# Reordering VectorE's, ACT's and SyncE's steps in the first round of block products, at the turns between token groups, and in the loads of x

## The chip, the cores and the metric

The kernel runs on one core of one Trainium2 chip. The metric is the device time of the whole program in microseconds (us); lower is better. A core has five engines with queues of their own, each of which works through its instructions in the order in which the program lists them: TensorE (PE, matrix products; its weight loads are shown as PEld), VectorE (DVE), ScalarE (ACT), GpSimd (POOL) and SyncE (SP, which here issues the DMA transfers).

## The reference

Block-sparse attention over q, k and v (4 batches, 8 heads, 768 positions, head size 64), and a two-layer network with a squared ReLU on its result:

```python
attn = softmax(where(mask, q @ k.T / 8, -1e9))       # mask: neighbours, edge blocks, sampled blocks
x = (attn @ v).transpose(0, 2, 1, 3).reshape(3072, 512)
h = x @ w_in                                         # w_in: 512 x 2048
r = maximum(h, 0)
g = s * (r * r) + b
out = g @ w_out                                      # w_out: 2048 x 512
```

The weights come as 64-bit floats. The kernel decodes each into a high and a low 32-bit part, and a product of two such operands is three matmuls: high by high, high by low, low by high.

## The kernel before, in words

**Stages.** Attention for all four batches comes first and spills x, transposed, to a DRAM tile `xd`. While it ends, the weights are decoded. Then comes the network. The tokens are cut into eight groups of 384, g = 0 to 7, two for each batch. Groups 0 and 1 go through the plain product: for each of 16 blocks f of 128 hidden columns, `mlp1` multiplies x by `w_in`, `relu`, `square`, `hidden_high` and `hidden_low` make the hidden block as a high and a low part (on ACT, ACT, ACT and DVE here), and `mlp2` multiplies it by `w_out` and adds it up in PSUM. These are 32 hidden blocks, i = 0 to 31. `mlp1(i)` writes PSUM bank i % 2, and `relu(i)` is what reads that bank.

**Block products.** Groups 2 to 7 are taken in pairs, a stage for each pair: s = 1, 2 and 3, with a = 2s and b = 2s + 1. Here x @ w_in is done in rounds p = 0 to 7, each of which makes hidden blocks p and p + 8 of both groups by seven block products instead of eight (a scheme of Strassen's kind). A round computes its products in the order n = 1, 2, 6, 7, 5, 3, 4. Product n multiplies a weight operand by an x operand:

| n | 1 | 2 | 6 | 7 | 5 | 3 | 4 |
|---|---|---|---|---|---|---|---|
| weight | A11 | A12 | S2 | S3 | S1 | S4 | A22 |
| x | B11 | B21 | T2 | T3 | T1 | B22 | T4 |

A11 to A22 are the quarters of the weight, S1 = A21 + A22, S2 = S1 - A11, S3 = A11 - A21, S4 = A12 - S2. The T's are differences and sums of parts of x in the same way: T3 = T3 - T1, T1 = T1 - T2, T2 = T2 + T3, T4 = T2 - T4, from four raw parts that are loaded into the tiles of that name. The T's and B's are made once for a stage, the S's once for a round. The change from one stage to the next is called a turn.

The products alternate between PSUM banks 0 and 1, so each waits until the product two places before it has been read. What reads them is on DVE, apart from product 1, which ACT copies (`m1`): product 2 is added to m1 and makes a hidden block (`take`: one add on DVE, then ReLU times itself on DVE), product 6 gives the partial sum u1, product 7 the partial sum u2, product 5 a hidden block and the partial sum u3, products 3 and 4 one hidden block each. `finish` makes a hidden block's high part on ACT (two steps) and its low part on POOL (line 425, the line of `hidden_low`). `out_block` is the `mlp2` of the oldest hidden block that waits in `fifo`: nine matmuls.

**Steps.** Everything else is a step with a short name, issued by `work(p, s, "...")` in the order in which the text lists it:

- `<T1`, `<B22`: load a part of x from `xd` (SP, 384 KB)
- `+T1`, `+S1`: add or subtract (DVE, line 543 or 546 for T, 541 for S)
- `wA12`: add the two parts of a weight quarter in a tile of its own (DVE, line 550). This is done only in stage 1.
- `>A12`: write that sum back over the high part of the weights (SP, line 553, 128 KB), once the products of this round have read it. `wA12` of the next round writes the same tile and so waits for this transfer; A11 and A21 likewise have one tile, A22 has two.
- `hT1`, `hS1`, `hB22`: high part of an operand (ACT, line 565)
- `lT1`, `lS1`, `lB22`: low part of it (DVE, line 567), after the high part
- `o4`: load an output weight block back from DRAM (SP, two transfers of 256 KB)

Up to hidden block 29 a planner orders the instructions: it is given for each operation its engine, a cost, a priority and what it depends on, and lays them out as a list for each engine. The list given to `early` puts the first steps of stage 1 into that plan at the lowest priority. From hidden block 30 on the order is written out by hand, in the loops printed below. `EARLY` holds the steps behind hidden blocks 30 and 31. `FIRST` holds those of stage 1's round 0, by product. `F_NOW` and `F_NEXT` hold what the rounds of stage 1 do for themselves and for the next round, `W_NOW` and `W_NEXT` the same for the weights in stages 2 and 3 (`W_NEXT[7]` also at the end of stage 1), `X_NOW` the x operands at the start of stages 2 and 3, `X_NEXT` what each round does for the x operands of the next stage. `BEHIND` holds the writes of stage 1, `BACK` the loads of the output weights.

Of the kernel before, what the change touches and what calls it, by code (L numbers as in the profile page):

```python
# [202 lines left out]
def kernel(  # L203
# [31 lines left out]
    NFC = DFF // P  # L235
# [295 lines left out]
    def get(s, n):  # L531
        g, c2 = FROM[n]
        xload(2 * s + g, c2, xsum_of(n))

    def add(p, s, n):

        if n[0] == "S":
            a11, a12, a21, a22 = (quarter(p, s, f"A{k}") for k in (11, 12, 21, 22))
            a, b, how = {"S1": (a21, a22, ALU.add), "S2": (wsum["S1"], a11, ALU.subtract),
                         "S3": (a11, a21, ALU.subtract), "S4": (a12, wsum["S2"], ALU.subtract)}[n]  # L540
            vec.tensor_tensor(out=wsum[n], in0=a, in1=b, op=how)
        elif n == "T4":
            vec.tensor_tensor(out=xsum[n], in0=xsum_of("T2"), in1=xsum[n], op=ALU.subtract)
        else:
            b, how = {"T3": ("T1", ALU.subtract), "T1": ("T2", ALU.subtract), "T2": ("T3", ALU.add)}[n]
            vec.tensor_tensor(out=xsum_of(n), in0=xsum_of(n), in1=xsum_of(b), op=how)

    def together(p, n):
        a, b = (quarter_part(p, n, part).bitcast(F32) for part in range(2))
        vec.tensor_tensor(out=put_together(p, n), in0=a, in1=b, op=ALU.add)  # L550
# [76 lines left out]
    with ExitStack() as es:  # L627
# [498 lines left out]
        for i, (kind, b, t, x) in enumerate(slots):  # L1126
# [31 lines left out]
            for j in range(nu):  # L1158
                n, ms_ = u + j, []
# [141 lines left out]

        for deps, what in (("", "<B11"), ("", "<B21"), ("", "<T1"), ("", "<T3"), ("", "<T2"), ("", "<T4"), ("<B11", "hB11"), ("hB11", "lB11"),
                           ("<B21", "hB21"), ("hB21", "lB21"), ("", "wA21"), ("", "wA22"), ("wA21 wA22", "+S1"), ("", "wA11"), ("+S1 wA11", "+S2"),
                           ("+S2", "hS2"), ("<T3 <T1", "+T3"), ("+T3 <T2", "+T1"), ("+T1", "+T2"), ("+T2", "hT2"), ("hS2", "lS2"), ("hT2", "lT2"),
                           ("+S2", "+S3"), ("+S3", ">A21")):
            early(deps, what)
        plan.run()


    W_NOW = {0: {1: "hS4"}, 1: {1: "lS3 hS4", 2: "lA22 lS4"}}  # L1310
    W_NOW.update({p: {1: "lS4 lA22"} for p in range(2, NFC // 2)})
    W_NEXT = {p: {1: "hA11", 2: "lA11 +S1 +S2 hA12", 6: "hS2", 7: "lA12 lS2 +S3", 5: "hS3 hS1 +S4", 4: "lS1 lS3 hS4 hA22"} for p in range(1, NFC // 2 - 1)}

    W_NEXT[7] = {1: "hA11", 2: "lA11 +S1 +S2 hA12", 6: "hS2", 7: "lA12 lS2", 5: "+S3 hS1", 4: "lS1 +S4 hS3 hA22"}
    W_NEXT[0] = {1: "hA11", 2: "lA11 hA12", 7: "lA12 +S1 +S2", 5: "hS2 hS1 +S3", 4: "lS2 lS1 +S4 hS3 hA22"}
    X_NOW = {1: "lT3 hT4 hB22", 2: "lT1 lS3", 7: "lB22 lS4 lT4", 5: "lA22"}
    X_NEXT = {2: {1: "<T1 <T3 <T2 <T4"}, 4: {2: "+T3", 7: "+T1"}, 5: {2: "+T2", 7: "+T4"},
              7: {1: "<B11", 2: "<B21", 6: "hB11", 7: "lB11 hT2 hB21", 5: "lT2 hT3", 3: "<B22", 4: "lB21 hT1"}}

    FIRST = {1: "lT1 lS1", 2: "hB22 hS4 lS4", 6: "lB22", 7: "hT4 lT4"}  # L1320
    F_NOW = {p: {1: "lS4"} for p in range(1, NFC // 2)}
    F_NEXT = {1: "wA21", 2: "wA22 +S1 wA11", 7: "+S2 hS2 +S3 >A21 wA12", 5: "+S4 hS3 hS1 lS2", 4: "lS1 lS3 hS4"}
    BEHIND = {1: ">A11", 2: ">A12", 4: ">A22"}
    BACK = {2: "o4", 3: "o5", 4: "o6", 5: "o7"}
    EARLY = {30: "hT3 lT3 hS3 lS3", 31: "<B22 hT1 hS1 +T4 wA12 +S4"}
    for i in range(NPL, NSUB):
        g, f = subs[i]
        mlp1(i)
# [5 lines left out]
        hidden_low(i)  # L1334
        work(0, S0, EARLY.get(i, ""))
        if i >= NSUB - LAG:
            fifo.append((i, None))
    for s in range(S0, B):
        a, b = 2 * s, 2 * s + 1
        for p in range(NFC // 2):  # L1340
            for n in (1, 2, 6, 7, 5, 3, 4):
                to = product(p, s, n)
                i = None
                if n in (2, 4) and len(fifo) >= 3 or n == 2 and s == S0 and p == 0:
                    out_block()
                if n == 1:
                    nc.scalar.copy(part_sums["m1"], to)
                elif n == 2:
                    i = take((a, p), to, part_sums["m1"], ALU.add)
                elif n == 6:  # L1350
                    vec.tensor_tensor(out=part_sums["u1"], in0=to, in1=part_sums["m1"], op=ALU.add)
                elif n == 7:
                    vec.tensor_tensor(out=part_sums["u2"], in0=to, in1=part_sums["u1"], op=ALU.add)
                elif n == 5:
                    i = take((b, p + 8), to, part_sums["u2"], ALU.add)
                    vec.tensor_tensor(out=part_sums["u3"], in0=to, in1=part_sums["u1"], op=ALU.add)
                elif n == 3:
                    i = take((b, p), to, part_sums["u3"], ALU.add)
                else:
                    i = take((a, p + 8), part_sums["u2"], to, ALU.subtract)  # L1360
                if s == S0:
                    work(p, s, BEHIND.get(n, ""))
                    work(p, s, BACK.get(p, "") if n == 1 else "")
                    work(p, s, FIRST.get(n, "") if p == 0 else F_NOW[p].get(n, ""))
                else:
                    if p == 0:
                        work(p, s, X_NOW.get(n, ""))
                    work(p, s, W_NOW[p].get(n, ""))
                if i is not None:
                    finish(i)  # L1370
                if s < B - 1:
                    work(p, s + 1, X_NEXT.get(p, {}).get(n, ""))
                if s == S0 and p < NFC // 2 - 1:
                    work(p + 1, s, F_NEXT.get(n, ""))
                elif s < B - 1 or p < NFC // 2 - 1:
                    work((p + 1) % (NFC // 2), s + p // (NFC // 2 - 1), W_NEXT[p].get(n, ""))
                if n == 7 and len(fifo) >= 2 or n == 5 and len(fifo) >= 3:
                    out_block()
# [75 lines left out]
```

## Time and profile before

| | |
|---|---|
| time, median of 3 runs | 809.35 us (807.5, 809.35, 809.81) |
| time of the profiled execution | 807.24 us |
| its span, first to last instruction | 805.2 us |
| busy: PE, PEld | 779.0 us (97%), 674.8 us (84%) |
| busy: DVE, ACT, POOL | 606.5 us (75%), 501.5 us (62%), 174.5 us (22%) |
| mean granted TensorE clock | 0.988 of full |
| first block product (stage 1, round 0) | at 408.34 us |
| stage 2, round 0 and stage 3, round 0 | at 541.73 us and 667.90 us |

Times within the profile are counted from the span's start. The rows of the profile name an engine, the line of the kernel, the operation, the tile written and the tile read, their shapes, and how often; a bracket tells how long the engine was idle ahead of the instruction and what ended the wait. A line can be that of a helper: all block products are line 583, all `mlp2` matmuls are lines 446 to 448, `take` is lines 593 and 594, m1 is line 1347, u1, u2 and u3 are lines 1351, 1353 and 1356. Tile names are those of the memory: `m` is a block product, `h` a product of `mlp1`, `o` one of `mlp2`; the operands of the T's and B's appear as `xT`, `xB`, `xt` or `wout`, those of the S's as `wop` or `win`, sums as `sum`, `whole` or `xrest`. PE's spans overlap, so that a stretch in which it is always busy need not be one in which it works at its peak.

### The profile page before, as it was taken

To read this page: it belongs to the slowest core of one execution; us is meant where nothing else is said; L and a number is where in the kernel's file an instruction comes from. 1 tells how busy PE (TensorE), PEld (TensorE's weight loads), DVE (VectorE), ACT (ScalarE), POOL (GpSimd) and SP (SyncE) were. 2 spreads that over 40 slices of the span, in tenths; PEclk is the share of its full clock that TensorE was granted. 3 is DMA by queue.
4 is the path that set the end of the run, shared out by engine and by line. 5 is a ranking of instruction groups with operands and counts; after the bars stand their busy time and mean duration, and the time that the engine had idled before them with its cause. 6 is when DMAs were issued, how large, how long until landed. Compare 5 with 4: busy or idle time off the path is not lost.

```text
span 805.2 us, 22023 instructions
## 1 busy us (share of the span) xinstructions
PE 779.0 (97%) x8352; PEld 674.8 (84%) x8352; DVE 606.5 (75%) x1528; ACT 501.5 (62%) x1190; POOL 174.5 (22%) x404
## 2 busy tenths in 40 slices
PE   7899998999999999999988999999999999999997
PEld 6587886888887899999867899998888888999986
DVE  5476777888888999998787678678667769766662
ACT  3576777787888887787864343467345457544542
POOL 5422133222400000000002232232223222322321
PEclk9899999999999999999999999999999999999999
DMA  9999797978677433543421422024000012000002
GB/s 251 251 236 310 223 262 233 245 202 235 187 228 248 143 123 105 194 146 115 143 86 66 138 82 70 26 86 144 14 0 1 1 40 93 7 1 1 1 0 79
DMA packets 89001, 100.99 MB, mean 125 GB/s; under 512 B 11584, under 2 KB 66368, under 8 KB 88896
## 3 DMA queue, kind: packets, MB, share of 16 engines
q1 hardware_dynamic: 88896, 99.59, 41.0%
q8 instruction: 66, 1.08, 0.6%
q14 instruction: 39, 0.32, 0.1%
HBM read 80.68 MB, written 14.68 MB: 118 GB/s over the span
## 4 chain that ended last, share of the span: by engine, by line
PE 90%; DMA 4%; DVE 2%; ACT 1%; SPq 1%; issue 1%; ACTq 0%; DVEq 0%
PE m L583 21%; PE o L447 10%; PE o L448 10%; PE o L446 10%; PE t L955 9%; PE xs L1000 5%; PE s L878 5%; PE xs L1014 3%; PE s L904 3%; PE h L404 3%; PE h L406 3%; PE h L405 3%; DMA kt<-in_k_seq_dram 2%; PE xs L989 1%; PE s L892 1%; PE xs L1026 1%
## 5 line engine op out<-in xcount | busy, mean ns | idle before, releaser
L425 POOL TENSOR_TENSOR hid<-hid,hid 128x384 fp32r<-128x384 f32 x96 | 102.9, 1073 | 476.3 <-ACT hid L601 475.9
L600 ACT ACTIVATE hid<-hid,sb_b,sb_s 128x384 f32<-128x384 f32 x96 | 68.0, 709 | 152.7 <-DVE hid L594 152.7
L931 ACT ACTIVATE ptile<-ptile,nm 128x352 f32<-128x352 f32 (+2 forms) x208 | 121.0, 584 | 33.9 <-DVE nm L919 33.3
L919 DVE CUSTOM_DVE_ANT_0 ptile<-s,ms 128x352 f32<-128x352 f32 x160 | 74.3, 521 | 27.1 <-PE s L904 26.5
L838 POOL COPY kg<-kt 128x128 f32 x264 | 63.6, 294 | 137.1 <-PE s L904 124.3
L583 PE MATMUL m<-wout,win 128*128 128x384 f32 x384 | 83.7, 339 | 2.0 <-ACT hid L409 1.9
L955 PE MATMUL t<-ident,ptile 128*128 128x128 f32 x608 | 80.4, 282 | 2.8 <-ACT ptile L931 2.6
L448 PE MATMUL o<-woutr,hid 128*128 128x512 f32 x192 | 75.9, 395 | 0.0
L447 PE MATMUL o<-woutr,hid 128*128 128x512 f32 x192 | 75.8, 395 | 0.0
L446 PE MATMUL o<-woutr,hid 128*128 128x512 f32 x192 | 74.6, 389 | 0.0
L955 PEld LDWEIGHTS t<-ident,ptile 128*128 128x128 f32 x608 | 67.2, 143 | 8.7 <-ACT ptile L931 3.5
L583 PEld LDWEIGHTS m<-wout,win 128*128 128x128 f32 x384 | 69.0, 188 | 6.2 <-ACT hid L409 2.7
L959 DVE COPY pt<-t 128x384 f32<-128x384 f32 (+1 forms) x104 | 56.3, 544 | 9.2 <-PE t L955 7.4
L583 PE MATMUL m<-xT,wop 128*128 128x384 f32 x288 | 58.8, 338 | 1.5 <-DVE hid L593 1.5
L961 ACT COPY pt<-t 128x384 f32<-128x384 f32 (+1 forms) x104 | 48.3, 474 | 17.0 <-PE t L955 16.2
L594 DVE SCALAR_TENSOR_TENSOR hid<-hid 128x384 f32<-128x384 f32 x96 | 55.3, 576 | 3.3
L583 PEld LDWEIGHTS m<-xT,wop 128*128 128x128 f32 x288 | 51.3, 188 | 4.5 <-DVE hid L593 1.8
L601 ACT CAST hid<-hid 128x384 fp32r<-128x384 f32 x96 | 49.3, 514 | 7.5 <-PE o L447 0.3
L567 DVE TENSOR_TENSOR win<-sum,win 128x256 fp32r<-128x256 f32 x48 | 31.8, 662 | 22.0 <-ACT win L565 22.0
L1000 PE MATMUL xs<-v,pt 128*64 128x64 f32 x1280 | 46.5, 225 | 1.8 <-issue 1.8
L448 PE MATMUL o<-wout,hid 128*128 128x512 f32 x120 | 48.1, 401 | 0.0
L1000 PEld LDWEIGHTS xs<-v,pt 128*64 128x64 f32 x1280 | 40.7, 138 | 8.8 <-issue 2.1
(186 smaller groups left out, 1754.5 us busy)
## 6 DMA issues: line engine op xcount, KB each, us to landing
vg<-in_v_dram SPq DMA_DIRECT2D x136, 128.0 KB, 3.5
v<-in_v_sta_dram SPq DMA_DIRECT2D x40, 256.0 KB, 4.2
kt<-in_k_seq_dram SPq DMA_DIRECT2D x16, 544.0 KB, 8.2
raw_i<-in_w_in_dram SPq DMA_DIRECT2D x16, 512.0 KB, 4.8
raw_o<-in_w_out_dram SPq DMA_DIRECT2D x16, 512.0 KB, 3.2
v<-in_v_dram SPq DMA_DIRECT2D x16, 384.0 KB, 4.8
xd<-xst SPq DMA_DIRECT2D x44, 128.0 KB, 3.8
out_dram<-ob SPq DMA_DIRECT2D x20, 256.0 KB, 2.0
```

The costliest lines, as they stand in the source:

```text
L425: (eng or nc.vector).tensor_tensor(out=htile(5 + i % 3), in0=t, in1=gh.bitcast(F32), op=ALU.subtract)
L446: nc.tensor.matmul(acc, gh[:, tsl], wout(f, 0), start=first, stop=False)
L447: nc.tensor.matmul(acc, gh[:, tsl], wout(f, 1), start=False, stop=False)
L448: nc.tensor.matmul(acc, gl[:, tsl], wout(f, 0), start=False, stop=last)
L583: nc.tensor.matmul(to, w_, x_, start=(c == 0 and k == 0), stop=(c == 1 and k == 2))
L600: nc.scalar.activation(t, t, AF.Identity, bias=sb_b, scale=sb_s)
L838: nc.gpsimd.tensor_copy(kg[:, m], kts[b][:, :, bass.ds(box["js"][m], BLK)])
L919: nc.vector.tensor_tensor_reduce(out=pt[:, :w], in0=sps.pop((n, g))[:, :w], in1=msk, scale=-scale, scalar=FMAX if g == 0 else nm[:, 0:1], ...
L931: nc.scalar.activation(pt[:, :w], pt[:, :w], AF.Exp, bias=nms[n][:, last:last + 1], scale=-1.0, accum_out=dns[i][:, g, j:j + 1])
L955: nc.tensor.transpose(tp[:, c, :], src[:, c * P:(c + 1) * P], ident)
L959: nc.vector.tensor_copy(to, src)
L1000: nc.tensor.matmul(xs[rows], pt[:, c, rows], vt[:, c, hp * D:(hp + 1) * D], start=(j == 0 and c == 0), stop=False, skip_group_check=True)
```

## The change

Seven tables and three lines of the loop change; what is computed stays as it is.

- T2's split (`hT2`, `lT2`) leaves the planner's list and goes behind hidden block 31. `+T4`, `wA12` and `+S4` leave the place behind hidden block 31 and go into `FIRST`, behind product 2 (`wA12`, `+S4`) and product 6 (`+T4`).
- `FIRST` is laid out anew: nothing behind product 1; `lT1` and `lS1` behind product 2, ahead of `wA12`, `+S4`, `hS4` and `hB22`; `lS4`, `+T4`, `hT4` behind product 6; `lB22` behind product 7; `lT4` behind product 5.
- What round 0 of stage 1 does for round 1 (`F_NEXT[0]`) goes behind products 5, 3 and 4, where it was spread from product 1 on. The other rounds keep their order.
- In stage 1 the write `>A11`, `>A12` or `>A22` is issued after `FIRST` or `F_NOW`, and the loads o4 to o7 go behind product 2 instead of product 1, so behind `>A12`.
- At the turns, `lS1` and `+S4` go from the end of round 7 to round 0's product 2 of the next stage, `lS3` ahead of `lT1` there, and `hS4` from product 1 to product 6.
- The loads of T1, T3, T2 and T4 for the next stage, which stood together behind product 1 of round 2, go behind product 5 of rounds 1, 2, 3 and 4.

```diff
-                           ("+S2", "hS2"), ("<T3 <T1", "+T3"), ("+T3 <T2", "+T1"), ("+T1", "+T2"), ("+T2", "hT2"), ("hS2", "lS2"), ("hT2", "lT2"),
+                           ("+S2", "hS2"), ("<T3 <T1", "+T3"), ("+T3 <T2", "+T1"), ("+T1", "+T2"), ("hS2", "lS2"),
                            ("+S2", "+S3"), ("+S3", ">A21")):
...
-    W_NOW = {0: {1: "hS4"}, 1: {1: "lS3 hS4", 2: "lA22 lS4"}}
+    W_NOW = {0: {6: "hS4"}, 1: {1: "lS3 hS4", 2: "lA22 lS4"}}
...
-    W_NEXT[7] = {1: "hA11", 2: "lA11 +S1 +S2 hA12", 6: "hS2", 7: "lA12 lS2", 5: "+S3 hS1", 4: "lS1 +S4 hS3 hA22"}
+    W_NEXT[7] = {1: "hA11", 2: "lA11 +S1 +S2 hA12", 6: "hS2", 7: "lA12 lS2", 5: "+S3 hS1", 4: "hS3 hA22"}
...
-    X_NOW = {1: "lT3 hT4 hB22", 2: "lT1 lS3", 7: "lB22 lS4 lT4", 5: "lA22"}
-    X_NEXT = {2: {1: "<T1 <T3 <T2 <T4"}, 4: {2: "+T3", 7: "+T1"}, 5: {2: "+T2", 7: "+T4"},
+    X_NOW = {1: "lT3 hT4 hB22", 2: "lS3 lT1 lS1 +S4", 7: "lB22 lS4 lT4", 5: "lA22"}
+    X_NEXT = {1: {5: "<T1"}, 2: {5: "<T3"}, 3: {5: "<T2"}, 4: {2: "+T3", 7: "+T1", 5: "<T4"}, 5: {2: "+T2", 7: "+T4"},
               7: {1: "<B11", 2: "<B21", 6: "hB11", 7: "lB11 hT2 hB21", 5: "lT2 hT3", 3: "<B22", 4: "lB21 hT1"}}
...
-    FIRST = {1: "lT1 lS1", 2: "hB22 hS4 lS4", 6: "lB22", 7: "hT4 lT4"}
+    FIRST = {2: "lT1 lS1 wA12 +S4 hS4 hB22", 6: "lS4 +T4 hT4", 7: "lB22", 5: "lT4"}
     F_NOW = {p: {1: "lS4"} for p in range(1, NFC // 2)}
-    F_NEXT = {1: "wA21", 2: "wA22 +S1 wA11", 7: "+S2 hS2 +S3 >A21 wA12", 5: "+S4 hS3 hS1 lS2", 4: "lS1 lS3 hS4"}
+    F_NEXT = {p: {1: "wA21", 2: "wA22 +S1 wA11", 7: "+S2 hS2 +S3 >A21 wA12", 5: "+S4 hS3 hS1 lS2", 4: "lS1 lS3 hS4"} for p in range(1, NFC // 2 - 1)}
+    F_NEXT[0] = {5: "wA21 wA22 +S1", 3: "wA11 +S2 hS2", 4: "+S3 >A21 hS3 hS1 lS2 wA12 +S4 lS3 lS1 hS4"}
...
-    EARLY = {30: "hT3 lT3 hS3 lS3", 31: "<B22 hT1 hS1 +T4 wA12 +S4"}
+    EARLY = {30: "hT3 lT3 hS3 lS3", 31: "<B22 hT2 lT2 hT1 hS1"}
...
                 if s == S0:
+                    work(p, s, FIRST.get(n, "") if p == 0 else F_NOW[p].get(n, ""))
                     work(p, s, BEHIND.get(n, ""))
-                    work(p, s, BACK.get(p, "") if n == 1 else "")
-                    work(p, s, FIRST.get(n, "") if p == 0 else F_NOW[p].get(n, ""))
+                    work(p, s, BACK.get(p, "") if n == 2 else "")
...
                 if s == S0 and p < NFC // 2 - 1:
-                    work(p + 1, s, F_NEXT.get(n, ""))
+                    work(p + 1, s, F_NEXT[p].get(n, ""))
```

## The prediction

> **What bounds the kernel now.** I read the page first, then the busy time cut into rounds of block products, then the order of instructions on each engine where a round is longer than its neighbours.
>
> ```profile
> span 805.2 us, 22023 instructions
> PE 779.0 (97%) x8352; PEld 674.8 (84%) x8352; DVE 606.5 (75%) x1528; ACT 501.5 (62%) x1190; POOL 174.5 (22%) x404
> ```
>
> TensorE (PE) is the bound, so only its gaps can be won. The profiled execution took 807.24 us, 2.04 more than its span. In the stretches below the columns are length, then busy us and instructions of PE, PEld, DVE, ACT and POOL, granted clock, DMA share and GB/s. The first four are rounds p = 0 to 3 of stage s = 1; then come the first rounds after the two turns; the last two stretches hold the clock dip.
>
> ```profile
> 408.34:430.10 21.76, 16.18 (x70) 13.25 (x71) 18.24 (x35) 16.31 (x32) 3.03 (x3) 0.93 0.27 97
> 430.10:445.93 15.83, 15.83 (x80) 14.26 (x79) 10.75 (x23) 6.26 (x13) 3.60 (x5) 0.99 0.10 34
> 445.93:463.20 17.27, 15.99 (x80) 14.10 (x78) 10.45 (x22) 5.83 (x13) 3.92 (x4) 1.00 0.48 153
> 463.20:478.90 15.70, 15.70 (x79) 14.14 (x78) 11.40 (x26) 7.28 (x15) 4.53 (x5) 1.00 0.20 68
> 541.73:557.98 16.25, 16.23 (x79) 14.04 (x78) 15.43 (x29) 12.25 (x26) 4.29 (x4) 1.00 0.24 86
> 667.90:684.12 16.22, 16.20 (x80) 14.04 (x78) 15.40 (x29) 12.22 (x26) 4.28 (x4) 1.00 0.22 82
> 423.40:426.80 3.40, 1.32 (x7) 1.34 (x8) 3.33 (x9) 3.37 (x8) 0.48 (x1) 1.00 0.56 200
> 426.80:430.20 3.40, 3.40 (x10) 2.63 (x9) 2.64 (x5) 2.10 (x5) 1.62 (x2) 0.53 0.22 75
> ```
>
> A round without a gap takes 15.70 us: seven products and four output blocks. Two rows price them.
>
> ```profile
> 436.51 0.39 PE L446 MATMUL o<-wout,hid 128*128 128x512 f32 x1
> 438.59 1.23 PE L583 MATMUL m<-xT,wop 128*128 128x384 f32 x6
> ```
>
> A block is 438.59 - 436.51 = 2.08, a product (15.70 - 4 x 2.08) / 7 = 1.05. Round 0 has only three blocks (two are queued when it begins), so it should take 7 x 1.05 + 3 x 2.08 = 13.6 us. It takes 21.76: **8.2 us are lost there**, 1.6 more in round 2 (17.27 against 15.70), 0.13 in round 1 and 0.5 at each turn. That is 11.0 us in all, and nothing else that the change touches has a gap. In round 0 the idle time stands here, ahead of products 2, 7 and 4 (order 1, 2, 6, 7, 5, 3, 4), and round 1 begins in the last row:
>
> ```profile
> 411.60 1.31 PE L583 MATMUL m<-wout,win 128*128 128x384 f32 x6 [1.95 <-ACT hid L409]
> 417.71 1.32 PE L583 MATMUL m<-xT,wop 128*128 128x384 f32 x6 [1.52 <-DVE hid L593]
> 425.48 1.28 PE L583 MATMUL m<-xT,win 128*128 128x384 f32 x6 [2.12 <-DVE sum L1356]
> 430.10 2.22 PE L583 MATMUL m<-wout,win 128*128 128x384 f32 x11
> ```
>
> 1.95 + 1.52 + 2.12 = 5.6 idle; after the last, PE runs at about half clock until 430.1 (0.53 granted), which is 1.6 more; the rest is start-up around the waits.
>
> **Part 1: T2's split leaves the planned list (hT2 on ACT, lT2 on DVE).** ACT's queue, with the matmul that ends the hidden block 30 and DVE's +T3:
>
> ```profile
> 403.66 0.41 ACT L565 CAST win<-sum 128x256 fp32r<-128x256 f32 x1 [3.46 <-DVE sum L541]
> 403.81 0.33 PE L406 MATMUL h<-x,win 128*128 128x384 f32 x1
> 403.87 0.95 DVE L546 TENSOR_TENSOR sum<-sum,sum 128x768 f32<-128x768 f32 x1
> 407.06 0.83 ACT L565 CAST wout<-sum 128x768 fp32r<-128x768 f32 x1 [3.00 <-DVE sum L546]
> 407.80 0.48 ACT L409 ACTIVATE hid<-h 128x384 f32<-128x384 f32 x1
> 410.03 0.83 ACT L565 CAST xT<-sum 128x768 fp32r<-128x768 f32 x1
> 410.76 0.40 ACT L565 CAST wop<-sum 128x256 fp32r<-128x256 f32 x1
> 411.07 0.48 ACT L409 ACTIVATE hid<-h 128x384 f32<-128x384 f32 x1
> 414.34 0.47 ACT L1347 COPY xrest<-m 128x384 f32<-128x384 f32 x1
> ```
>
> hT2 (407.06) idles ACT for 3.00 us waiting for +T2, with relu 30 queued behind it, though block 30 is done at 404.14. Without it relu 30 goes at 404.2. Its block's four ACT steps take 410.03 - 407.80 = 2.23: hT3 at 406.4 (its input +T3 is there from 404.82), hS3 at 407.2, relu 31 at 407.5 (now 411.07). Product 2 waits for relu 31's bank, so the first wait goes. Then 2.23 for block 31, 0.73 for hT2 at its new place and 1.04 for hT1 and hS1: the copy of product 1 starts at 411.5 and ends at 411.95, where now it starts at 414.34. Cover for hT2: product 6, its reader, comes after product 2 and a block, at 408.15 + 2 x 1.05 + 2.08 = 412.3 (product 1 starts once the block before it ends, 0.2 sooner than now); hT2 runs 409.7 to 410.55, lT2 on DVE then 0.95 to 411.5. That is 0.8 us of slack, and the copy, which product 6's bank waits for, has 0.35.
>
> **Part 2: the order FIRST.** DVE's steps as they stand, with the start-to-start times that I use:
>
> ```profile
> 413.90 0.95 DVE L543 TENSOR_TENSOR sum<-sum,sum 128x768 f32<-128x768 f32 x1
> 414.77 0.42 DVE L550 TENSOR_TENSOR sum<-win 128x256 f32<-128x256 f32 x1
> 415.22 0.43 DVE L541 TENSOR_TENSOR sum<-sum,sum 128x256 f32<-128x256 f32 x1
> 415.57 0.95 DVE L567 TENSOR_TENSOR xT<-sum,xT 128x768 fp32r<-128x768 f32 x1
> 417.10 0.55 DVE L593 TENSOR_TENSOR hid<-m,xrest 128x384 f32<-128x384 f32 x1
> 417.69 0.56 DVE L594 SCALAR_TENSOR_TENSOR hid<-hid 128x384 f32<-128x384 f32 x1
> 418.17 0.42 DVE L567 TENSOR_TENSOR win<-sum,win 128x256 fp32r<-128x256 f32 x1
> 420.10 1.37 DVE L567 TENSOR_TENSOR xB<-xB 128x768 fp32r<-128x768 f32 x1
> 421.39 0.55 DVE L1353 TENSOR_TENSOR xrest<-m,sum 128x384 f32<-128x384 f32 x1
> ```
>
> Wide step 0.87 (413.90 to 414.77), narrow 0.35 (0.45 if the next one reads it), a product's add 0.59, its square 0.48, lB22 1.29, a partial sum 0.47. Nothing is removed here: +T4, wA12, +S4, lT1, lS1 and wA21, ahead of product 2's sum at 417.10 now, go behind it. The sum then starts when the copy lands, 412.0. From there, added up in the new order: square 412.6; lT1 413.05; lS1 413.9; wA12 414.25; +S4 414.7; u1 415.05; lS4 415.5; +T4 415.85; u2 416.75; lB22 417.2; product 5's sum 418.5; its square 419.1; u3 419.55; lT4 420.0; wA21, wA22, +S1 to 422.0; product 3's sum 422.0; wA11, +S2; product 4's at 423.9; then six narrow steps of round 1 and its lS4, and round 1's product 2 at 427.8.
>
> PE against that: products 1 and 2 at 408.15 and 409.2, block, product 6 at 412.3, product 7 at 413.4, block, product 5 at 416.6 (needs u1, 415.6: hidden). Product 3 is ready at 417.65 but needs lB22, 417.2 + 1.29 = 418.5: **0.9 idle**. Product 4 is ready at 419.6 but needs lT4, 420.0 + 0.95 = 421.0: **1.4 idle**. Then a block, and round 1 begins at 421.05 + 1.05 + 2.08 = 424.2 instead of 430.10: **5.9 us won**. ACT hides behind this: hS4 waits for +S4 to 415.15 with hB22 and product 2's finish behind it; hB22 ends at 416.3, before lB22. The last steps listed for round 1 (+S3 to hS4, now all behind product 4) are read by its products 6, 5 and 3, from 428.4 on: hidden. >A21 goes out on SP behind >A22, when product 4 ends (422.1), and must have read its tile before wA21 of round 2 writes it, near 427.5: hidden too, with 5 us for 128 KB, when 384 KB in a stack took 6.4 (below).
>
> The longest gap of 1.4 us leaves over 2 us busy in any 3.4 us, against 1.32 ahead of the dip, so I take the clock as full. The Trainium skill, "TensorE: Matmul & The Clock Gate", section "Part 1: The HAM clock gate", puts the half clock after an idle window of about 3.4 us; the trace differs, since its window of the dip follows one with 1.32 us of work in it. By the page's rule the new gaps cost no clock either.
>
> What can stretch the chain is POOL:
>
> ```profile
> 426.32 1.02 POOL L425 TENSOR_TENSOR hid<-hid,hid 128x384 fp32r<-128x384 f32 x1 [5.67 <-ACT hid L601]
> 426.50 1.25 DVE L594 SCALAR_TENSOR_TENSOR hid<-hid 128x384 f32<-128x384 f32 x1
> ```
>
> The square takes 1.25 beside POOL and 0.56 alone: 0.69 lost. Three such meetings are to be had between 417.5 and 427 (POOL follows each finish). The first is in lB22's 1.37 already; two add 1.4 to round 1's product 2, which then passes PE's need for it at 429.5 by about 0.3; **0.5 us off**, between 0 and 1.5.
>
> **Part 3: BEHIND ahead of BACK, x loads spread.** Round 2 loses its 1.57 here:
>
> ```profile
> 457.94 0.43 DVE L550 TENSOR_TENSOR sum<-win 128x256 f32<-128x256 f32 x1 [4.29 <-DMA win<-sum]
> ...
> sum<-xd SPq DMA_DIRECT2D x4, 384.0 KB, 6.4
> ```
>
> wA12 waits for the write >A12, which stands on SP behind o4's two loads and four x loads (six transfers, 2 MB). Now >A12 goes ahead of o4, and only one x load, of the round before, is in front of it. The wait goes, **1.57 won** (0 if >A12 still lands late, no more than 1.57). Round 1's 0.13 goes with the dip. o4 to o7, now behind product 2, are used two rounds later: nothing. BEHIND's swap with F_NOW's lS4 changes no queue, as one is SP's and the other DVE's. The x loads go in rounds 1 to 4; T2's and T4's first readers stand at product 7 of the next round, their issue at product 5: in round 1 these begin at 436.51 - 1.05 = 435.46 and at 438.59, so 15.70 - 3.1 = 12.6 us lie between, twice the 6.4 that four stacked loads took.
>
> **Part 4: the turns.** PE's weight load waits there:
>
> ```profile
> 547.45 0.64 PEld L583 LDWEIGHTS m<-xT,wop 128*128 128x128 f32 x4 [0.28 <-DVE wop L567]
> 555.78 0.19 PEld L446 LDWEIGHTS o<-wout,hid 128*128 128x128 f32 x1 [0.34 <-ACT ob L452]
> ```
>
> The first is lS3, now ahead of lT1 (0.87 earlier): 0.28 won at each of two turns. lS1 and +S4 move behind it, 0.7 us of DVE; DVE is 15.43 of 16.25 busy, but both leave the same round's stretch, so product 2's sum starts that much earlier and u1 where it did. hS4 at product 6 delays no ACT step that PE needs. The second wait stays. **0.56 won**, between -1.0 (u1 0.5 late each time) and 1.07.
>
> **Sum:** 5.9 - 0.5 + 1.57 + 0.13 + 0.56 = 7.7, so 807.24 - 7.7 = 799.5 against the profiled execution. That one was quicker than the three runs (807.5, 809.35, 809.81; median 809.35, which would give 801.7); the mean of the four is 808.5, hence 801.
>
> **Rivals.**
> A. All gaps close: DVE catches up and products 3 and 4 wait for nothing. Then 11.0 goes: 796.2 to 798.4. Against it: 18.24 us of DVE work in round 0, now to be done in less time.
> B. DVE becomes the bound of rounds 0 and 1. POOL's meetings fall on the chain from 412 to 424, three at 0.69, and one gap grows until the clock halves for a window (1.6 as now): 7.7 - 2.1 - 1.6 = 4.0, so 804.5. The square's 1.25 speaks for it. In the Trainium skill, "SBUF — State Buffer", section "SBUF: two separate sides", VectorE and GpSimd hold a shared port pair as an exclusive lock for a whole instruction; the square, which ends only 0.4 after POOL, agrees.
> C. Round 0 doesn't shrink, since ACT is held elsewhere ahead of relu 31 (hT3 or the output copies). Then 1.57 + 0.56 remains: 806.4. Against it: +T3 ends on DVE at 404.82. From the mean of four that is 0.26%, no change that can be told.
> D. Slower: an x load lands late. T2's and T4's readers stand in DVE's queue ahead of the sums that free PE's banks. DVE's wait of 4.29 cost PE 1.57, so PE bears 2.7; a landing above 12.6 + 2.7 = 15.3 us costs, four times over. At 18 us the 7.7 and the 2.4 of a measurable loss are used up; at 18.5 it is 813. Nothing in the 6.4 speaks for it.
>
> **How the numbers follow.** Forecast 0.57, A 0.12, B 0.19, C 0.07, D 0.05. About 0.3% (2.4 us, the spread of the runs) can be told from no change: the forecast, A and B are faster (0.88), C is the same, D slower. The range goes from A's floor, 796.5, to C's edge at 806.5; D and half of C lie outside.
>
> **What would show it.** Right: relu 31 near 407.5; round 1 beginning near 424; no clock under 0.9 after 405; round 2 at 15.7; wA12 waiting for no DMA. Wrong: PE waits ahead of products 3 or 4 above 2 us, a second half-clock window, or DVE waiting for the x loads.

## The result and the profile after

The changed kernel takes 802.75 us (median of 20 runs, 799.86 to 810.38), the kernel before 809.67 us (20 runs in turn with it, 803.91 to 812.59). The ratio is 0.9928, with a 95% interval of 0.991 to 0.9947. The medians differ by 6.9 us. 801.0 was forecast, between 796.5 and 806.5.

The profiled execution of the changed kernel took 805.12 us, with a span of 803.1: only 2.1 less than before's 805.2. But its first block product stands at 412.48, where before's stands at 408.34. Those 4.1 us belong to attention and the plain products ahead of the block products; the runs below show that they aren't the change's. From the first block product to the end it is 803.1 - 412.48 = 390.6 us, against 805.2 - 408.34 = 396.9: **6.24 us won where the change is**. This measure ("the rest") is the one used from here on.

The same stretches as in the prediction, in the changed kernel: rounds 0 to 3 of stage 1, then the first rounds after the two turns (length, then busy us and instructions of PE, PEld, DVE, ACT and POOL, granted clock, DMA share, GB/s).

```profile
412.48:428.30 15.82, 14.39 (x70) 12.34 (x69) 13.88 (x25) 10.84 (x21) 2.74 (x2) 1.00 0.36 132
428.30:445.53 17.23, 16.25 (x80) 14.01 (x78) 15.30 (x33) 9.16 (x19) 5.00 (x5) 1.00 0.16 56
445.53:461.23 15.70, 15.70 (x79) 14.13 (x78) 10.66 (x24) 6.60 (x14) 4.22 (x5) 1.00 0.27 93
461.23:476.94 15.71, 15.71 (x79) 14.13 (x78) 10.68 (x24) 6.61 (x14) 4.24 (x5) 1.00 0.27 93
539.77:556.03 16.26, 15.97 (x80) 14.09 (x78) 15.28 (x29) 12.41 (x26) 5.41 (x4) 1.00 0.23 84
665.97:682.03 16.06, 15.97 (x79) 14.09 (x78) 14.74 (x29) 12.21 (x26) 5.08 (x4) 1.00 0.23 83
```

Against the rows of before: round 0 21.76 to 15.82, won 5.94; round 1 15.83 to 17.23, **lost 1.40**; round 2 17.27 to 15.70, won 1.57; first turn 16.25 to 16.26, lost 0.01; second 16.22 to 16.06, won 0.16. The sum is 6.26 of the 6.24.

Where round 0 still waits, ahead of products 3 and 4, and what round 1 waits for, in the order of time:

```profile
422.62 1.15 PE L583 MATMUL m<-xB,win 128*128 128x384 f32 x5 [0.36 <-DVE xB L567]
424.47 0.41 PE L583 MATMUL m<-xT,win 128*128 128x384 f32 x1 [0.70 <-DVE sum L1357]
425.24 1.14 PE L583 MATMUL m<-xT,win 128*128 128x384 f32 x5 [0.36 <-DVE xT L567]
433.91 0.45 PE L583 MATMUL m<-wout,win 128*128 128x384 f32 x1 [0.98 <-ACT xrest L1348]
422.62 0.82 PEld L583 LDWEIGHTS m<-xB,win 128*128 128x128 f32 x5 [0.62 <-DVE xB L567]
424.44 0.19 PEld L583 LDWEIGHTS m<-xT,win 128*128 128x128 f32 x1 [1.01 <-ACT ob L452]
425.24 0.82 PEld L583 LDWEIGHTS m<-xT,win 128*128 128x128 f32 x5 [0.61 <-DVE xT L567]
433.91 0.19 PEld L583 LDWEIGHTS m<-wout,win 128*128 128x128 f32 x1 [1.42 <-ACT xrest L1348]
```

The weight load is the better gauge of what a wait costs, since PE's rows overlap: 0.62 + 1.01 + 0.61 = 2.24 is what round 0 takes above the 13.6 us of its work, and 1.42 is nearly all of the 1.53 that round 1 takes above 15.70. The rows also name the work that is late: lB22 for product 3, then u3 (line 1357), which frees product 4's bank, and lT4 for the rest of product 4. The releaser `ACT ob` in the second weight-load row was done at 423.98, ahead of u3 at 424.33; PE's own row names u3.

Round 1's wait is the new one. It stands ahead of product 6, whose bank is free when ACT has copied product 1. These are the rows of DVE, ACT and POOL that lead to it:

```profile
429.57 1.37 POOL L425 TENSOR_TENSOR hid<-hid,hid 128x384 fp32r<-128x384 f32 x1 [3.17 <-PE m L583]
429.97 1.24 DVE L541 TENSOR_TENSOR sum<-whole 128x256 f32<-128x256 f32 x1
431.47 1.29 POOL L425 TENSOR_TENSOR hid<-hid,hid 128x384 fp32r<-128x384 f32 x1 [0.54 <-ACT hid L601]
431.92 1.12 DVE L541 TENSOR_TENSOR sum<-sum,sum 128x256 f32<-128x256 f32 x1
433.07 0.41 ACT L565 CAST win<-sum 128x256 fp32r<-128x256 f32 x1 [1.07 <-DVE sum L541]
433.39 0.47 ACT L1348 COPY xrest<-m 128x384 f32<-128x384 f32 x1
434.31 0.55 DVE L593 TENSOR_TENSOR hid<-m,xrest 128x384 f32<-128x384 f32 x1
```

Two low parts on POOL stretch two of DVE's additions for round 1 (+S3 and +S4, line 541) from 0.42 to 1.24 and 1.12. hS4 on ACT waits 1.07 for +S4, and the copy of product 1 is queued behind hS4. So a step that no product needs soon holds up, in ACT's queue, one that PE needs now.

### The profile page after: what moved, and what is told of

It reads as the page before. It is cut to its first block, busy times and chain, and to the rows that moved or that the text cites. A ratio compares the mean times of both kernels' runs of the same rounds, so it can differ in the third digit from the quotient of the medians.

```text
span 803.1 us, 22021 instructions
## 1 busy us (share of the span) xinstructions
PE 777.3 (97%) x8352; PEld 674.1 (84%) x8352; DVE 606.0 (75%) x1528; ACT 501.7 (62%) x1190; POOL 178.2 (22%) x404
## 4 chain that ended last, share of the span: by engine, by line
PE 83%; DVE 5%; DMA 4%; ACT 3%; SPq 2%; issue 2%; ACTq 0%; DVEq 0%
PE m L583 19%; PE o L447 10%; PE o L448 10%; PE o L446 10%; PE t L955 8%; PE xs L1000 5%; PE s L878 5%; PE xs L1014 3%; PE h L404 3%; PE h L406 3%; PE h L405 3%; DMA kt<-in_k_seq_dram 2%; PE s L904 2%; PE xs L989 1%; PE s L892 1%
## 5 line engine op out<-in xcount | busy, mean ns | idle before, releaser
L425 POOL TENSOR_TENSOR hid<-hid,hid 128x384 fp32r<-128x384 f32 x96 | 106.1, 1106 | 468.5 <-ACT hid L601 457.3
L593 DVE TENSOR_TENSOR hid<-m,xrest 128x384 f32<-128x384 f32 x48 | 26.5, 552 | 30.2 <-issue 25.6
```

The costliest lines, as they stand in the source:

```text
L425: (eng or nc.vector).tensor_tensor(out=htile(5 + i % 3), in0=t, in1=gh.bitcast(F32), op=ALU.subtract)
```

## Experiments: the parts of the change

All of them are the changed kernel with the edit shown (- the changed kernel, + the experiment; ... stands for text left out). Each was run once, so the lengths of the rounds and the rest are compared, not the total times.

**T2's split back in the planner's list** (part 1 undone):

```diff
-   ... ("+T1", "+T2"), ("hS2", "lS2"),
+   ... ("+T1", "+T2"), ("+T2", "hT2"), ("hS2", "lS2"), ("hT2", "lT2"),
-    EARLY = {30: ..., 31: "<B22 hT2 lT2 hT1 hS1"}
+    EARLY = {30: ..., 31: "<B22 hT1 hS1"}
```

> The changed kernel with one part undone: T2's split (hT2, lT2) goes back into the planner's list, all else new. Theory (ACT's queue held relu 30 and relu 31, and so product 2): relu 31 starts some 3 us later than in the changed kernel (there 0.7 us ahead of product 1's start, here 2.5 us or more behind it), PE waits 1.5 to 2.5 us ahead of product 2 again, and round 0 takes 17.0 to 18.5 us where the changed kernel took 15.82. Rival (FIRST's order alone won round 0): round 0 stays within 0.5 us of 15.82.

Measured: round 0 19.11, more than the 17.0 to 18.5 expected; round 1 17.24; the rest 393.9, 3.3 more than the changed kernel. The wait of 1.95 for relu 31 is back, to the hundredth:

```profile
414.83 1.34 PE L583 MATMUL m<-wout,win 128*128 128x384 f32 x6 [1.95 <-ACT hid L409]
```

The clock fell as well, right behind that wait. These are the 3.41 us of half clock, and the 3.41 us ahead of them:

```profile
412.79:416.20 3.41, 1.46 (x8) 1.37 (x8) 1.85 (x3) 3.28 (x8) 0.00 (x0) 1.00 0.11 38
416.20:419.61 3.41, 3.41 (x9) 2.65 (x8) 2.06 (x4) 2.91 (x6) 0.00 (x0) 0.50 0.06 23
```

So part 1 removes its wait, as forecast. What the part is worth by itself can't be read off cleanly, as the 3.3 hold a clock dip (3.41 us at half clock, so 1.7 us of TensorE's time) that the same wait did not bring on in the kernel before (last section).

**The old FIRST and F_NEXT[0]** (part 2 undone, T2's split where the change puts it):

```diff
-    FIRST = {2: "lT1 lS1 wA12 +S4 hS4 hB22", 6: "lS4 +T4 hT4", 7: "lB22", 5: "lT4"}
+    FIRST = {1: "lT1 lS1", 2: "hB22 hS4 lS4", 6: "lB22", 7: "hT4 lT4"}
-    F_NEXT[0] = {5: "wA21 wA22 +S1", ...}
-    EARLY = {30: ..., 31: "<B22 hT2 lT2 hT1 hS1"}
+    F_NEXT[0] = F_NEXT[1]
+    EARLY = {30: ..., 31: "<B22 hT2 lT2 hT1 hS1 +T4 wA12 +S4"}
```

> The changed kernel with the order of round 0 undone: FIRST and round 0's steps for round 1 as before, +T4, wA12 and +S4 again behind hidden block 31; T2's split stays at its new place behind hidden block 31. Theory (the order is a second, separate part): +T4, wA12, +S4, lT1, lS1 and wA21 stand ahead of product 2's sum on DVE again, some 3 us, so PE waits for DVE ahead of products 7 and 4 and round 0 takes 18 to 21 us against 15.82; round 1 goes back to 15.7 to 16.0, since hS4 no longer stands ahead of product 1's copy there. Rival (T2's split did it all): round 0 within 1 us of 15.82.

Measured: round 0 19.64, round 1 15.70, the rest 392.9, 2.3 more than the changed kernel. The two waits of before for DVE, 1.52 and 2.12 there, are back:

```profile
419.90 1.32 PE L583 MATMUL m<-xT,wop 128*128 128x384 f32 x6 [1.71 <-DVE hid L593]
427.67 1.30 PE L583 MATMUL m<-xT,win 128*128 128x384 f32 x6 [2.09 <-DVE sum L1357]
```

Behind the second wait the clock is halved here too (0.50 from 428.80 to 432.21). The two undone parts cost 3.3 and 2.3, 5.6 together, where rounds 0 and 1 of before take 37.59 - 33.05 = 4.54 more than the changed kernel's. The parts don't add up, and the clock is one reason: each of the two kernels has a dip of its own, before has one in all. What each part is worth without a dip, these runs don't show.

**The order of BACK and of the x loads** (part 3, two kernels):

```diff
-                    work(p, s, BACK.get(p, "") if n == 2 else "")
+                    work(p, s, BACK.get(p, "") if n == 1 else "")
```

> The changed kernel with the loads o4 to o7 again behind product 1, ahead of the write >A12; the x loads stay spread. If the stack of four x loads was what made >A12 late, round 2 stays at 15.70 us and wA12 waits for no DMA; >A12 lands 1 to 2 us later than in the changed kernel. If the two o loads were what made it late, wA12 waits again and round 2 takes 16.5 us or more.

```diff
-    X_NEXT = {1: {5: "<T1"}, 2: {5: "<T3"}, 3: {5: "<T2"}, 4: {2: "+T3", 7: "+T1", 5: "<T4"}, ...
+    X_NEXT = {2: {1: "<T1 <T3 <T2 <T4"}, 4: {2: "+T3", 7: "+T1"}, ...
```

> The changed kernel with the four x loads together behind product 1 of round 2 again; o4 to o7 stay behind product 2, behind >A12. The four x loads then stand ahead of >A12 on SP (1.5 MB). Theory (the x loads are the weight of the stack): wA12 waits 1 to 3 us and round 2 takes 15.7 to 16.8 us. Rival (the position of the o loads alone freed it): wA12 waits for no DMA and round 2 takes 15.70.

Measured: with BACK ahead of `>A12` again, round 2 takes 15.70 and the rest 390.6: no cost. The write goes out 2.78 us after the round's start instead of 2.12, and wA12 waits for no transfer. With the four x loads stacked again, round 2 takes 16.17: 0.47. DVE then waits 3.2 us for the write, in the list of waits (us in total, times, longest):

```profile
DVE sum L550 <- DMA win<-sum: 3.2, 1, 3.2
```

With both, as before has it, DVE waited 4.29 and the round lost 1.57. So the stack is the cause, and the o loads only make it worse: DVE's slack takes up most of the first 3.2 us of wait, and between these two kernels PE loses as much as DVE waits longer (1.1 more wait, 1.1 more loss).

**The old turns** (part 4 undone):

```diff
-    W_NOW = {0: {6: "hS4"}, ...
+    W_NOW = {0: {1: "hS4"}, ...
-    W_NEXT[7] = {..., 4: "hS3 hA22"}
-    X_NOW = {1: "lT3 hT4 hB22", 2: "lS3 lT1 lS1 +S4", ...
+    W_NEXT[7] = {..., 4: "lS1 +S4 hS3 hA22"}
+    X_NOW = {1: "lT3 hT4 hB22", 2: "lT1 lS3", ...
```

> The changed kernel with the steps at the two turns as before (lS1 and +S4 at the end of round 7, lT1 ahead of lS3, hS4 behind product 1). Theory (the turn is bound by the output copy that ACT does behind product 5's finish, hS2 and hS1, and lS3's wait was covered by it): the 0.28 wait for lS3 ahead of product 7 comes back, and the first rounds of stages 2 and 3 take 16.1 to 16.3 us each, no more than 0.2 from the changed kernel's 16.26 and 16.06. Rival (the prediction's 0.28 a turn was real and something else took it): they take 16.4 to 16.6.

Measured: the turns take 16.57 and 16.21, the rest 391.2. The wait ahead of product 7 is back:

```profile
543.30 0.98 PE L583 MATMUL m<-xT,wop 128*128 128x384 f32 x4 [0.30 <-DVE wop L567]
```

Against the changed kernel the part is worth 0.31 and 0.15. But before itself had 16.25 at the first turn, not 16.57, with the same order of steps. The difference enters ahead of the turn: the last sum of stage 1 stands 0.34 later on DVE, 1.46 us ahead of the turn instead of 1.80. Before, then the changed kernel:

```profile
539.93 0.55 DVE L593 TENSOR_TENSOR hid<-xrest,m 128x384 f32<-128x384 f32 x1
538.31 0.55 DVE L593 TENSOR_TENSOR hid<-xrest,m 128x384 f32<-128x384 f32 x1 [0.25 <-issue]
```

The turns are at 541.73 and 539.77. What DVE waits for in these 0.25 us no row names; every profile of the changed kernel and its variants has the gap, except the two that take low parts off POOL (below), whose first turns take 16.03 and 16.06 us. So at the first turn part 4 won about 0.3, and this gap took it back.

## Experiments: what round 1 and the turns lose

**+S4 out of the crowd.** If hS4 behind +S4 is what holds the copy, +S4, hS4 and lS4 of round 1 behind its product 2 should free it:

```diff
+    F_NOW[1] = {2: "+S4 hS4 lS4"}
-    F_NEXT[0] = {..., 4: "+S3 >A21 hS3 hS1 lS2 wA12 +S4 lS3 lS1 hS4"}
+    F_NEXT[0] = {..., 4: "+S3 >A21 hS3 hS1 lS2 wA12 lS3 lS1"}
```

> The changed kernel with +S4 and hS4 for round 1 of stage 1 taken from behind product 4 of round 0 and put, with lS4, behind product 2 of round 1. Theory (hS4 in ACT's queue, waiting for +S4 on DVE, holds the copy of round 1's product 1, and so product 6): the 0.98 wait ahead of product 6 goes, round 1 takes 15.7 to 16.2 us against 17.23, round 0 stays at 15.8. Rival (DVE as a whole is too late in round 1): PE waits for DVE there instead, at product 7 or 3, and round 1 stays above 16.8.

Measured: round 1 16.78, 0.45 less than 17.23; more was expected. The wait ahead of product 6 is gone, but POOL now meets the next steps of DVE, lS3 and lS1, and product 7 waits for product 2's sum behind them:

```profile
429.24 1.29 POOL L425 TENSOR_TENSOR hid<-hid,hid 128x384 fp32r<-128x384 f32 x1 [0.54 <-ACT hid L601]
429.58 1.56 DVE L567 TENSOR_TENSOR wop<-sum,wop 128x256 fp32r<-128x256 f32 x2
432.00 1.16 PE L583 MATMUL m<-xT,wop 128*128 128x384 f32 x5 [0.24 <-DVE hid L593]
```

So ACT's queue was only the last link: DVE's sums themselves are late, and the next two runs show why.

**POOL's part left out, and done twice.** The low parts of hidden blocks 32 to 35, the first four of stage 1, are left out of the result in the first kernel, and made twice, with the same result, in the second:

```diff
-        hidden_low(i, gps)
+        if not NSUB <= i < NSUB + 4:
+            hidden_low(i, gps)
```

> The changed kernel without POOL's low part of the four hidden blocks of round 0 of stage 1, which leaves these four low parts out of the result. Theory (POOL's steps stretch DVE's): in the first 20 us from product 1 no DVE step of 256 columns takes over 0.5 us (1.12 and 1.24 in the changed kernel), +S4 ends 1.2 to 2.5 us sooner, and the wait ahead of round 1's product 6 falls from 0.98 to 0 to 0.3, round 1 to 15.7 to 16.5. Rival (DVE is late by its number of steps alone): the wait stays above 0.7.

```diff
         hidden_low(i, gps)
+        if NSUB <= i < NSUB + 4:
+            hidden_low(i, gps)
```

> The changed kernel with POOL doing the low part of the four hidden blocks of round 0 of stage 1 twice, with the same result. Theory (POOL's steps stretch DVE's): DVE's steps beside the added ones take 0.5 to 0.8 longer each, the wait ahead of round 1's product 6 grows by 0.7 to 2.5 us, and rounds 0 and 1 together take 34 to 36 us against 33.05. Rival: they stay within 0.4 of 33.05.

Measured, rounds 0 and 1 without that work on POOL:

```profile
411.12:426.74 15.62, 14.42 (x71) 12.36 (x69) 13.64 (x27) 11.65 (x22) 0.00 (x0) 1.00 0.37 133
426.74:442.45 15.71, 15.71 (x80) 14.13 (x79) 13.02 (x31) 8.29 (x18) 2.39 (x3) 1.00 0.18 61
```

and with it done twice:

```profile
407.16:423.51 16.35, 14.60 (x71) 12.19 (x69) 14.41 (x24) 10.79 (x20) 5.01 (x4) 1.00 0.36 129
423.51:443.00 19.49, 16.37 (x79) 14.13 (x80) 17.55 (x34) 9.23 (x19) 6.99 (x7) 1.00 0.15 48
```

Round 1: 15.71, 17.23, 19.49 with none, one and two times POOL's work on these four blocks; without it no addition of line 541 in the first 20 us takes over 0.43 us. That POOL causes the whole of round 1's loss is shown: nothing but POOL's work differs, and DVE's busy time in round 1 goes from 13.02 to 15.30 to 17.55 us for 31, 33 and 34 instructions. DVE hardly does more, it is held. The Trainium skill, "SBUF — State Buffer", section "SBUF: two separate sides", says that VectorE and GpSimd share a port pair under an exclusive lock, which a VectorE operation with two inputs in SBUF needs too; the trace agrees (0.42 becomes 1.24 beside a POOL step).

**The same low parts on DVE.** If being held costs DVE more than the work, DVE could do it itself, each low part one product later. +S4 and hS4 are late as above, lS4 one product later still:

```diff
-        hidden_low(i, gps)
+        if not NSUB <= i < NSUB + 4:
+            hidden_low(i, gps)
...
+    F_NOW[1] = {2: "+S4 hS4", 6: "lS4"}
+    LOW = {(0, 5): 0, (0, 3): 1, (0, 4): 2, (1, 7): 3}
-    F_NEXT[0] = {..., 4: "+S3 >A21 hS3 hS1 lS2 wA12 +S4 lS3 lS1 hS4"}
+    F_NEXT[0] = {..., 4: "+S3 >A21 hS3 hS1 lS2 wA12 lS3 lS1"}
...
+                if s == S0 and (p, n) in LOW:
+                    hidden_low(NSUB + LOW[p, n])
```

> The changed kernel with the low parts of round 0's four hidden blocks on DVE, one product later each, instead of POOL, and with round 1's +S4 and hS4 behind its product 2 and lS4 behind product 6. Theory (a POOL step costs DVE more, 0.7 us, than the 0.47 us of doing its work): no step of 256 columns above 0.5 us in rounds 0 and 1, no wait for product 1's copy, round 0 in 15.6 to 16.0 us and round 1 in 15.7 to 16.0. Rival (four more steps on the fullest engine cost as much): round 0 at 16.2 or more or round 1 at 16.6 or more.

Measured: round 0 15.86, round 1 16.75, the rest 390.1: as good as +S4 late alone (16.78, 390.2), no better. Up to product 2's sum no step is stretched, but DVE now has the work: a product waits for its sum, and an output block for the low part that it now makes:

```profile
426.41 1.31 PE L583 MATMUL m<-wout,win 128*128 128x384 f32 x6 [0.23 <-DVE hid L593]
435.82 0.19 PEld L448 LDWEIGHTS o<-woutr,hid 128*128 128x128 f32 x1 [0.67 <-DVE hid L425]
```

In these two orders round 1 pays the same, whether POOL holds DVE or DVE does POOL's work.

**The turn, one product later.** In the changed kernel product 7's wait is gone, and yet the first turn is no shorter. The first matmul of the last block of round 0 waits longer than before (0.61 against 0.34), for ACT's output copies. ACT, in the changed kernel, with PE's weight load:

```profile
551.39 0.71 ACT L600 ACTIVATE hid<-hid,sb_b,sb_s 128x384 f32<-128x384 f32 x1 [2.46 <-DVE hid L594]
552.19 0.52 ACT L601 CAST hid<-hid 128x384 fp32r<-128x384 f32 x1
552.61 0.40 ACT L565 CAST win<-sum 128x256 fp32r<-128x256 f32 x1
552.91 0.40 ACT L565 CAST wop<-sum 128x256 fp32r<-128x256 f32 x1
553.22 1.55 ACT L452 COPY ob<-o 128x512 f32<-128x512 f32 x3
553.85 0.19 PEld L446 LDWEIGHTS o<-wout,hid 128*128 128x128 f32 x1 [0.61 <-ACT ob L452]
```

The copies are queued behind hS2 and hS1 of the next round, and these behind product 5's finish, which waits for DVE, where +S1 and +S2 stand ahead of product 5's sum. So round 0 should do its steps for round 1 one product later:

```diff
-    W_NEXT[0] = {..., 7: "lA12 +S1 +S2", 5: "hS2 hS1 +S3", 4: "lS2 lS1 +S4 hS3 hA22"}
+    W_NEXT[0] = {..., 7: "lA12", 5: "+S1 +S2", 3: "hS2 hS1 +S3", 4: "lS2 lS1 +S4 hS3 hA22"}
```

> The changed kernel with the next round's +S1 and +S2 behind product 5's sums instead of ahead of them, and hS2 and hS1 behind product 3, in the first rounds of stages 2 and 3. Theory (those rounds are bound by DVE's chain up to product 5's sum and ACT's steps behind it, which hold the copies of the output and so the last block): product 5's sum starts some 0.8 us sooner, the copies too, the wait of the block's first matmul goes, and these two rounds take 15.7 to 15.9 us each against 16.26 and 16.06. Rival (the copies wait for PE's own last output block): no change, 16.0 to 16.3.

Measured: both turns at a full round, 15.71 and 15.70 instead of 16.26 and 16.06, and the rest 389.7, 0.9 less. The first of them, and its copies:

```profile
537.78:553.49 15.71, 15.71 (x79) 14.13 (x78) 14.14 (x27) 12.21 (x25) 5.74 (x5) 1.00 0.29 106
549.88 1.56 ACT L452 COPY ob<-o 128x512 f32<-128x512 f32 x3
```

The copies now come right after the finish, 549.88 - 537.78 = 12.10 us from the round's start instead of 553.22 - 539.77 = 13.45, and no matmul waits. So the chain to the copies, DVE's product-5 sum and ACT's queue behind it, is what the turns lose by. The edit moves DVE's steps and ACT's together; the share of each is not told apart.

**Both repairs, and the changed kernel again.** Five steps of round 1 leave the crowd, together with the later steps at the turns; and the changed kernel once more beside it, six runs each. In the first, lS1 of round 1 stands behind the `+S1` of round 2, so this one low part is made from round 2's sum and the result is wrong: this kernel shows what the order costs and is none to use. The instructions are the same in number and kind.

```diff
     F_NOW = {p: {1: "lS4"} for p in range(1, NFC // 2)}
+    F_NOW[1] = {2: "wA12 +S4 hS4", 6: "lS1 lS4"}
-    F_NEXT[0] = {..., 4: "+S3 >A21 hS3 hS1 lS2 wA12 +S4 lS3 lS1 hS4"}
+    F_NEXT[0] = {..., 4: "+S3 >A21 hS3 hS1 lS2 lS3"}
-    W_NEXT[0] = {..., 7: "lA12 +S1 +S2", 5: "hS2 hS1 +S3", ...
+    W_NEXT[0] = {..., 7: "lA12", 5: "+S1 +S2", 3: "hS2 hS1 +S3", ...
```

> The changed kernel with two more moves: for round 1 of stage 1, wA12, +S4 and hS4 go behind its product 2 and lS1, lS4 behind its product 6 (they stood behind product 4 of round 0), and at the turns round 0's steps for round 1 begin one product later (+S1 +S2 behind product 5). Theory (round 1's loss is DVE work that POOL stretches ahead of product 2's sum; with five steps out of that stretch, four of them on DVE, 1.6 us of DVE work goes from in front of that sum): round 1 15.8 to 16.3 instead of 17.2, both turns 15.7 instead of 16.26 and 16.06, 388.7 to 389.4 from the first product on (the changed kernel: 390.6), ratio to the kernel before 0.990 to 0.9915. Rival (the stretched steps only move to the next wait, as with +S4, hS4 and lS4 alone, where round 1 came to 16.78): round 1 16.6 or more, 389.5 or more from the first product on, of which only the turns are won, ratio 0.9917 to 0.992.

> The changed kernel as it is, again, on the same chip as the version with two more moves. Theory: round 0 15.8, round 1 17.2, turns 16.26 and 16.06, 390.6 from the first product on, ratio to the kernel before 0.991 to 0.9947; the part ahead of the first product comes out differently (407 to 413 us, as in the runs so far), with the same order of instructions. Rival (the part ahead of the first product does depend on the change, which profiled it at 412.5): again at 412 to 413.

Measured: 800.96 us with both repairs (6 runs, ratio to the kernel before 0.9918, interval 0.9895 to 0.994), 801.32 us for the changed kernel again (6 runs, 0.9929, interval 0.9903 to 0.9954), 806.96 us for the kernel before (11 runs). The intervals overlap. From the first block product on the profiles have 389.7, where 388.7 to 389.4 was expected, and 390.7; the 0.9 between them is what the turns won (15.70 twice, against 16.24 and 16.05). The first block product of the changed kernel stands at 407.82 this time, so its 412.48 in the first profile was not the change's.

On round 1 the two kernels say nothing, against both theories, since the clock fell in round 0 in both. Rounds 0 and 1 of the repaired kernel:

```profile
409.37:426.74 17.37, 15.95 (x70) 13.70 (x69) 15.35 (x28) 12.31 (x23) 3.02 (x3) 0.90 0.33 122
426.74:442.43 15.69, 15.69 (x80) 14.11 (x79) 14.41 (x30) 7.60 (x16) 4.48 (x5) 1.00 0.18 59
```

and of the changed kernel in its second profile:

```profile
407.82:425.21 17.39, 15.96 (x71) 13.62 (x70) 15.37 (x28) 12.30 (x23) 3.05 (x3) 0.90 0.33 122
425.21:440.90 15.69, 15.69 (x80) 14.10 (x78) 13.77 (x30) 7.70 (x16) 4.66 (x5) 1.00 0.18 59
```

The second pair is the same program as in the first section, and rounds 0 and 1 still take 33.08 us together, 33.05 there. The dip costs 1.57 in round 0 and gives DVE the time that it lacks in round 1, where PE never waits; in the first profile that wait cost 1.53. That the two are so nearly equal is chance: the repaired kernel, whose sums come sooner, takes 33.06 with the dip as well. Product 2's sum of round 1 starts 21.83 us after the first product in the first profile (434.31 - 412.48) and 21.80 in this one. In the repaired kernel it starts at 20.52. Without a dip product 7 would need that sum by 15.82 + 3 x 1.05 + 2.08 = 21.05, and it would end at 20.52 + 0.55 = 21.07; so round 1 should come to about 15.8. That is an estimate from these rows, for an order with one wrong low part; no profile shows it without the dip.

## Why the prediction was nearly right, and what was mis-sized

The sum of the parts was 7.7 us, and 6.24 us came. By its steps:

- **What bounds the kernel.** PE's gaps, and those that closed were where the prediction put them. This held; the gap that opened, in round 1, it priced too low.
- **Part 1.** relu 31 was put 0.7 ahead of product 1 and stands 0.68 ahead (411.80 to 412.48). The wait for it is gone, and comes back when hT2 goes back.
- **Part 2, the new order.** Round 0 was forecast at 15.9 and takes 15.82. The idle time was put at 0.9 ahead of product 3 and 1.4 ahead of product 4, 2.3 in all; it is 0.62 and 1.01 + 0.61, 2.24 in all. That the first matmul of product 4 would wait for u3, and only the rest for lT4, was not said. lB22 ran 0.95 rather than the 1.29 assumed, and product 5's square 0.79 rather than 0.56: two errors that partly cancel.
- **The clock taken as full.** It was so in the first profile, and was not in the second, which has the half-clock window that the prediction named as a sign of being wrong. "Over 2 us busy in any 3.4 us" counts the longest gap alone: the two forecast gaps, 0.9 and 1.4, lie one product (1.05) apart and would leave about 1.1. Measured, the emptiest 3.4 us hold 1.97 us of work in the first profile (from 422.25) and in the second (from 417.59). That the first kept its clock was luck, and so was it that the dip in the second cost no more than the wait that it replaced.
- **POOL's meetings, 0.5 off: the term that was mis-sized.** With the 0.13 of the dip the forecast for round 1 was 15.83 - 0.13 + 0.5 = 16.2; it took 17.23, 1.03 more. The stretch was priced by the square (0.69 lost); +S3 and +S4 lose 0.82 and 0.70, and the pair wA21 and wA22 in round 0 about 0.8 (1.57 us against 0.75 without POOL). Behind this the step failed in its path too: product 2's sum was taken as the only one that PE waits for, and hS4 as harmless because its product comes late. But hS4 waits for +S4 with the copy of product 1 queued behind it. At hS4 in round 0 that question was asked, at the hS4 of round 1 it was not.
- **Part 3, 1.57.** Round 2 went from 17.27 to 15.70, and wA12 waits for no transfer. Exact, though the forecast did not say that spreading the x loads would do by itself.
- **Part 4, 0.56.** 0.15 came. lS3's wait went at both turns; "the second wait stays" was wrong: it grew from 0.34 to 0.61 at the first and stands at 0.41 at the second. At the first turn DVE's gap at the end of stage 1, which no row of before shows, took the gain; at the second the growth took a part of it. What is late next was named and not followed to what it waits for, DVE's sum of product 5 and ACT's queue behind it.
- **The sum**: 1.03 for round 1 and 0.41 for the turns make 1.44 of the 1.46 that are missing.

Of the rivals, A (all gaps close) and C (round 0 doesn't shrink) are excluded by round 0's 15.82, and D (a late x load) by rounds 2 and 3 at 15.70: DVE waits for no x load. B's mechanism, DVE as the bound of rounds 0 and 1 through POOL, is what happens, at less than a third of B's price: that was 2.1 + 1.6 = 3.7 us on top of the forecast's 0.5, and 1.03 came on top of it.

## What to carry to other kernels

When steps are moved later on a crowded engine, price the new place and not the step: the additions that cost 0.42 us where they stood cost 1.24 beside another engine's work. For each moved step follow the queue of the engine that reads it, and ask what stands behind that reader, even if the reader's own result is wanted late. And compare the stage that was changed, from a common event in it, rather than spans: here the spans differ by 2.1 us, the stage by 6.24.

## What the runs showed of the hardware

**The same gap halves the clock in one execution and not in another.** In these profiles the granted clock changes only in steps of 3.41 us whose places are fixed within an execution, and lie elsewhere in the next one. In the first profile of the changed kernel, the step that holds the gaps ahead of product 4, and the next:

```profile
423.80:427.22 3.42, 2.38 (x11) 1.99 (x12) 3.38 (x7) 1.31 (x3) 1.18 (x1) 1.00 0.66 235
427.22:430.63 3.41, 3.41 (x18) 2.87 (x17) 3.31 (x7) 2.07 (x4) 1.06 (x1) 1.00 0.25 87
```

In the second, the same program, one step holds the gaps ahead of both products:

```profile
417.65:421.06 3.41, 2.04 (x9) 1.50 (x10) 3.38 (x7) 2.79 (x6) 1.63 (x2) 1.00 0.56 202
421.06:424.48 3.42, 3.42 (x10) 2.89 (x9) 3.32 (x7) 0.89 (x2) 0.67 (x1) 0.50 0.33 110
```

The gaps are the same, but 2.38 us of the step were busy in one and 2.04 in the other, and the clock behind it is 1.00 and 0.50. So it is with the wait of 1.95 for relu 31: 1.46 us busy in its step in the experiment above, and half clock behind it; in the kernel before 1.72, and full clock:

```profile
409.91:413.32 3.41, 1.72 (x9) 1.63 (x10) 1.85 (x3) 3.31 (x8) 0.00 (x0) 1.00 0.11 38
413.32:416.74 3.42, 2.87 (x14) 2.02 (x12) 3.28 (x6) 3.42 (x8) 0.00 (x0) 1.00 0.17 66
```

The Trainium skill, "TensorE: Matmul & The Clock Gate", section "Part 1: The HAM clock gate", says that the activity window of about 3.4 us runs freely, so that it depends on its phase what falls into it. That agrees with these pairs. But the page asks for an idle window, and no window here was idle: up to 2.04 us of 3.41 were busy. Over the 14 profiles, from 100 to 790 us, every step at full clock with 1.55 us of work or less was followed by half clock, every one with 2.07 or more by full clock; between these both happened, five times each. Gaps of 0.6 to 1.0 us close together therefore have a price with a chance, and the clock of one execution isn't evidence of an order's merit.

**The part ahead of the first block product varies by itself.** It took from 407.16 to 412.79 us in the profiles here, and 412.48 and 407.82 in two profiles of the same program. That spread of 5.6 us is nearly as much as the change wins.

**POOL is held as well.** By its rows, which are rough on POOL, a low part takes 1.02 us alone and 1.18 to 1.56 beside DVE's steps in rounds 0 and 1 of the changed kernel.
